# A tuned kernel's stated order of steps is written anew, and the zero products fill TensorE's whole array

## The chip, the core and the metric

The kernel runs on one core of a Trainium2 chip. The core has five engines that run side by side: TensorE (PE, matrix products), VectorE (DVE), ScalarE (ACT), GpSimd (POOL) and SyncE (SP, which here only issues DMAs). Each engine executes its own instructions strictly in the order in which they stand, and an instruction that needs another engine's result waits for it on a semaphore. The metric is the device time of one execution in microseconds (us). Three runs of the kernel before gave 550.38, 552.77 and 553.58 us, so the median is 552.77.

## What is computed

The reference has two stages. The first is a delta rule, for 4 batches and 8 heads, 768 steps and a head width of 48 (`k_n` is the normalised key):

```
y[t]   = q[t] @ state
v_old  = k_n[t] @ state
state += beta[t] * outer(k_n[t], v[t] - v_old)
```

The second takes `x`, which is y with the heads side by side (4 x 768 tokens of 384), and adds a two-layer block to it: `xn = (x - mean)/sqrt(var + 1e-6) * g_ln`, and `out = x + max(xn @ w_ch1, 0) @ w_ch2`, with `w_ch1` of 384 x 1536 and `w_ch2` of 1536 x 384. Everything is float32.

## The kernel before, in words

The 768 steps are cut into 12 chunks of 64 (`C = 64`, `NCH = 12`). A chunk of the delta rule becomes a set of small products of 48 or 64 rows, 32 products to a step, one for each pair of batch and head. They can be told in the profile by their lines:

- L766 (`products`): the chunk's products of keys with keys (`G`) and of queries with keys (`P`);
- L718 and L733 (`first_inverse`, steps `E1` to `E5` and `Z1` to `Z5`): chunk 0's triangular inverse by five rounds of products, each round passing through VectorE (L723 copies under a mask, L683 transposes) and ScalarE (L677 copies);
- L884, L889 (`blocks_join`), L921, L927 (`join`): the inverses of the later chunks, 32 x 32 products that put together what VectorE worked out row by row (`rows_inverse`, L850 and L857);
- L974 (`state` in `recur`: `ks`, `qs`), L993, L998, L1010 and L1029 (`u`), L1046 (`state_up`), L1036 (`out_y`): the recurrence from chunk to chunk. Each chunk reads the state that the chunk before has left.

A layer norm follows (L1080 to L1092) and the chunk's 256 tokens are turned (L1124, or through a DMA). The two-layer block (`mlp`) then runs as large products with 128 rows and 128 columns: L1296 and L1318 for chunk 0 and, in the first layer, chunks 1 and 2; L1229 (`eleven`, the first layer of chunks 3 to 11 with eleven block products instead of twelve) and L1394 (`seven`, the second layer of chunks 1 to 11 with seven for eight). Their sums and differences are done by VectorE (L1251, L1412), GpSimd (L1380, L1419) and ScalarE (L1248).

The order of all this is no scheduler's work at run time. Every step is recorded with `add` in the object `line` (class `Line`): an engine, a function that issues the step's instructions, and what it reads and writes. There are 3154 steps. `Line.emit` then calls them in the order that the string `ORDER` states, number by number, and asserts that no step comes before one that it needs. `a:b` in the string is a range of steps, and `z` is no step but a call of `line.filler`. With `in_this_order` that order becomes the order of each engine's queue, DMAs included.

`line.filler` is the function `zeros` (L1471 to L1473): two products whose result nobody reads, put into columns 384 to 512 of bank `f_[0]`. In the kernel before there are 20 `z`. Their stationary operand is `pmask` (128 rows, 64 columns), so their result covers 64 partitions. The bank `f_[0]` is also one of the banks of `first_inverse`, which uses its columns 0 to 256.

What sets the order around the change is thus the string alone. A product in float32 is issued as two weight loads and two matmuls, a transpose (L576, L1124) as one of each.

Of the kernel before, what the change touches and what calls it, by code (L numbers as in the profile page):

```python
# [16 lines left out]
C = 64  # L17
# [42 lines left out]
8 55 54 47 65 53 59 1 9 10 61 50 52 11 51 2 5 12 32 57 13 74 23 41 29 0 56 66 35 58 37 6 7 48 38 63 75 39 64 42 68 45 76 43 67 91 40 251 92 81 77 80  # L60
93 84 250 36 100 85 33 30 101 102 31 4 34 103 18 78 26 14 17 69 19 15 104 82 105 86 83 87 94 98 27 71 95 28 96 88 99 106 79 97 16 89 107 90 109 24 25
209 113 110 108 111 310 114 112 115 118 204 208 213 119 125 116 72 120 205 z 121 123 122 126 70 128 z 127 117 258 21 124 20 235 22 130 259 129 252 233
256 49 131 46 221 136 255 132 223 44 206 253 142 135 133 137 260 134 138 308 141 222 143 144 139 224 140 238 145 146 632 73 633 148 152 240 234 147
309 236 154 158 149 254 153 151 60 150 257 159 155 160 157 393 156 237 396 161 163 z 219 162 307 3 168 207 169 z 167 210 217 164 392 173 165 211 170
175 166 212 171 261 229 176 178 z 174 172 177 402 244 179 180 321 262 263 186 215 181 320 311 182 242 397 187 192 264 185 265 319 188 184 312 266 183
239 322 189 193 194 190 241 191 401 313 195 196 391 314 246 389 267 200 268 214 315 z z 400 197 243 203 269 218 198 394 270 202 271 201 220 395 272
225 273 274 333 z 248 399 216 275:277 398 278 245 316 334 279 199 280 317 336 281 282 62 331 283 318 338 247 323 357 332 324 z 249 325 341 326 335 z
342 227 284 337 285 327 286 362 287 339 346 355 z z 340 347 328 226 288 343 289 329 348 290 344 356 345 330 291 353 390 367 292 349 293 422 z 294 295
351 352 296 230 350 297 463 231 423 z 354 298 232 425 464 570 358 465 228 462 572 571 365 574 424 363 467 426 469 573 364 360 359 576 366 427 575 466
# [12 lines left out]
690 790 z z 789 691 791 692 792 926 793 564 1187 794 795 1170 890 796 927 891 1188 800 797 902 1183 565 798 1373 801 799 928 693 802 1067 803 807 z z  # L82
z z 694 804 805 1563 930 806 808 1073 810 809 566 695 878 569 892 929 568 1071 567 903 696 1075 697 931 698 1565 699 964 1189 1369 905 700 966 1380
# [123 lines left out]
def kernel(  # L207
# [13 lines left out]
    nc = tc.nc  # L221
# [20 lines left out]
    def sb(name, shape, dt=FP32):  # L242
        return const.tile(shape, dt, name=name)
# [38 lines left out]
    ident = sb("ident", [128, 128])  # L282
    pmask = sb("pmask", [128, C])
# [26 lines left out]
    f_ = [psum.tile([128, 512], FP32, name=f"f{i}") for i in range(4)]  # L310
# [1160 lines left out]
    def zeros():  # L1471
        for _ in range(2):
            nc.tensor.matmul(f_[0][0:C, 384:512], pmask, pmask[:, 0:1].to_broadcast([128, 128]))  # L1473
# [139 lines left out]
```

## Time and profile before

| | before |
|---|---|
| median of three runs | 552.77 us |
| the profiled execution | 553.62 us |
| its span, first to last instruction | 551.9 us |
| mean granted clock of TensorE | 0.974 |
| TensorE matmuls, weight loads | 10088, 10088 |
| busy: TensorE, VectorE, GpSimd, ScalarE | 517.1, 360.4, 254.6, 197.2 us |
| instruction packets for TensorE (queue q8) | 79, 1.29 MB |

The profile is a page and a trace of one execution. Times in it start at the first instruction. Its second part cuts the span into 40 equal slices and gives a digit for each, the busy share in tenths; the row PEclk is the clock that TensorE was granted. A row of waits names the engine and line that waited, what released it, the total, how often and the longest. "issue" as a releaser means that the engine waited for nothing that the profile shows. In rows in order of time the first number is the start, the second the duration of the group; matmuls overlap, so the time that a step takes is read from start to start. "x64" counts matmuls in a trace row.

### The profile page before, as it was taken

To read this page: it belongs to the slowest core of one execution; us is meant where nothing else is said; L and a number is where in the kernel's file an instruction comes from. 1 tells how busy PE (TensorE), PEld (TensorE's weight loads), DVE (VectorE), ACT (ScalarE), POOL (GpSimd) and SP (SyncE) were. 2 spreads that over 40 slices of the span, in tenths; PEclk is the share of its full clock that TensorE was granted. 3 is DMA by queue.
4 is the path that set the end of the run, shared out by engine and by line. 5 is a ranking of instruction groups with operands and counts; after the bars stand their busy time and mean duration, and the time that the engine had idled before them with its cause. 6 is when DMAs were issued, how large, how long until landed. Compare 5 with 4: busy or idle time off the path is not lost.

```text
span 551.9 us, 23155 instructions
## 1 busy us (share of the span) xinstructions
PE 517.1 (94%) x10088; PEld 471.2 (85%) x10088; DVE 360.4 (65%) x884; ACT 197.2 (36%) x496; POOL 254.6 (46%) x399
## 2 busy tenths in 40 slices
PE   7778996999989998998999899999999999999996
PEld 4667884779978897997998899998899998999996
DVE  5668468981789736998758788659858334444331
ACT  5576644341323324223314324223422234132220
POOL 6134184537723697466272444460251551335443
PEclk9687899999999999999999899999999999999999
DMA  9884869178454686452673255761534510303101
GB/s 160 251 182 88 243 146 156 24 172 132 69 71 84 190 135 68 90 102 47 178 107 62 34 107 136 177 90 23 103 60 97 119 19 4 89 1 87 30 1 29
DMA packets 195973, 54.67 MB, mean 99 GB/s; under 512 B 186136, under 2 KB 189344, under 8 KB 195872
## 3 DMA queue, kind: packets, MB, share of 16 engines
q1 hardware_dynamic: 190112, 40.39, 38.4%
q10 hardware_dynamic: 3552, 9.63, 5.6%
q0 software_dynamic: 2208, 3.17, 3.9%
q8 instruction: 79, 1.29, 1.0%
q14 instruction: 22, 0.18, 0.1%
HBM read 36.38 MB, written 16.78 MB: 96 GB/s over the span
## 4 chain that ended last, share of the span: by engine, by line
PE 74%; DVE 10%; issue 5%; DMA 4%; SPq 3%; POOL 1%; ACT 1%; POOLq 0%; ACTq 0%; DVEq 0%
PE f L1229 23%; PE f L1394 22%; PE f L1296 6%; SPq L357 3%; PE two L766 3%; PE f L1318 3%; DVE xb L857 3%; DVE tmp L850 2%; PE by L1036 2%; PE two L1029 2%; PE by L974 2%; PE two L974 2%; PE two L1046 1%; PE f L1473 1%; DMA words<-in_moe_w_ch_dram 1%
## 5 line engine op out<-in xcount | busy, mean ns | idle before, releaser
L1380 POOL TENSOR_TENSOR h_all<-h_all 128x256 f32<-128x256 f32 x99 | 75.7, 770 | 58.0 <-PE f L1394 53.5
L1394 PE MATMUL f<-w_sb,h_all 128*128 128x192 f32 x396 | 95.8, 331 | 1.4 <-issue 1.1
L1229 PE MATMUL f<-xnt,w_sb 128*128 128x128 f32 x648 | 89.8, 280 | 1.3 <-issue 1.0
L1394 PE MATMUL f<-words,h_all 128*128 128x192 f32 x396 | 86.2, 329 | 0.0
L1419 POOL TENSOR_TENSOR words<-h_all 128x128 f32<-128x128 f32 x66 | 30.3, 477 | 120.4 <-ACT h_all L1248 114.6
L1229 PEld LDWEIGHTS f<-xnt,w_sb 128*128 128x128 f32 x648 | 81.6, 194 | 2.9 <-ACT rstd L1086 1.3
L1251 DVE TENSOR_TENSOR h_all<-f,h_all 128x256 f32<-128x256 f32 x135 | 56.1, 419 | 41.1 <-PE f L1229 33.4
L850 DVE TENSOR_TENSOR tmp<-xb,gb 128x60 f32<-128x60 f32 (+19 forms) x170 | 67.4, 396 | 4.5
L1394 PEld LDWEIGHTS f<-w_sb,h_all 128*128 128x128 f32 x396 | 66.4, 190 | 3.3 <-issue 2.0
L857 DVE TENSOR_TENSOR xb<-xb,tmp 128x60 f32<-128x60 f32 (+19 forms) x170 | 65.7, 387 | 3.9
L1394 PEld LDWEIGHTS f<-words,h_all 128*128 128x128 f32 x396 | 67.2, 190 | 0.8 <-POOL h_all L1380 0.2
L357 POOL DMA_DIRECT2D tb<-in_k_dram x64 | 41.9, 658 | 24.2 <-DVE tmp L850 17.0
L1296 PE MATMUL f<-xnt,w_sb 128*128 128x256 f32 x216 | 49.8, 384 | 0.9 <-ACT h_all L1305 0.9
L1296 PEld LDWEIGHTS f<-xnt,w_sb 128*128 128x128 f32 x216 | 40.2, 190 | 7.3 <-ACT h_all L1305 1.3
L1412 DVE TENSOR_TENSOR o<-f,x 128x192 f32<-128x192 f32 x33 | 11.4, 353 | 50.2 <-PE f L1394 40.0
L1248 ACT ACTIVATE h_all<-f 128x256 f32<-128x256 f32 x54 | 20.5, 382 | 65.0 <-PE f L1229 31.7
L1394 PE MATMUL f<-w_sb,words 128*128 128x192 f32 x132 | 32.7, 332 | 1.4 <-DVE o L1412 1.4
L1248 ACT ACTIVATE h_all<-h_all 128x256 f32<-128x256 f32 x54 | 21.4, 412 | 23.0 <-DVE h_all L1251 22.7
L550 POOL TENSOR_TENSOR w_sb<-words 128x768 uint32<-128x768 uint32 (+1 forms) x11 | 15.1, 1374 | 21.1 <-DVE words L537 14.8
L1305 ACT ACTIVATE h_all<-f 128x256 f32<-128x256 f32 x36 | 13.1, 383 | 33.0 <-PE f L1296 33.0
L1394 PEld LDWEIGHTS f<-w_sb,words 128*128 128x128 f32 x132 | 22.8, 190 | 2.0 <-DVE o L1412 1.7
L1074 ACT COPY x<-by 128x384 f32<-128x384 f32 x23 | 10.1, 481 | 30.9 <-PE by L1036 18.1
(235 smaller groups left out, 924.0 us busy)
## 6 DMA issues: line engine op xcount, KB each, us to landing
words<-in_moe_w_ch_dram ACTq DMA_DIRECT2D x10, 768.0 KB, 8.2
gd<-gsb SPq DMA_DIRECT2D x11, 512.0 KB
v<-in_v_dram SPq DMA_DIRECT2D x24, 192.0 KB, 3.7
out_dram<-o SPq DMA_DIRECT2D x48, 96.0 KB, 2.3
kr<-in_k_dram SPq DMA_DIRECT2D x46, 96.0 KB, 3.3
xld<-xlt SPq DMA_DIRECT2D x9, 384.0 KB, 2.5
xnt<-xld SPq DMA_DIRECT2D x36, 96.0 KB, 3.1
gb<-gd SPq DMA_DIRECT2D x40, 64.0 KB, 3.6
```

What stands on the lines that cost most here:

```text
L357: add(eng, cost, lambda: QUEUE[eng].dma_start(out=out_, in_=in_), r, w, bulk=n * ns / 16e3, **kw)
L766: nc.tensor.matmul(pair[hp][half(e ^ (hp & n)), (g * NP + j) * C : (g * NP + j + 1) * C], kt[drows(hp), l], rt[drows(hp), i],)
L850: lambda j=j, n=n, w=w, t=t: nc.vector.tensor_tensor(out=t, in0=xv[:, 0:n, j : j + 1].to_broadcast([128, n, w]), in1=gv[:, j : j + 1, j + ...
L857: "DVE", dve(n * w), lambda t=t, rest=rest: nc.vector.tensor_tensor(out=rest, in0=rest, in1=t, op=ALU.subtract),
L974: nc.tensor.matmul(dst[half(e), hp, j], src[drows(hp), (e if n else key_half(c, hp, e)) * GP + j], s_all[drows(hp), e, j], start=(n == 0 o ...
L1229: nc.tensor.matmul(wide(p[:, 128 * n : 128 * n + 128]), w[:, f : f + 128], r, start=start and n == 0, stop=stop, skip_group_check=True)
L1248: add("ACT", act(256), lambda: nc.scalar.activation(to[0], p, ACTF.Relu), pk, to[1])
L1251: add("DVE", dve(256), lambda: nc.vector.tensor_tensor(out=to[0], in0=ps(p), in1=y[0], op=op), [*pk, *y[1]], to[1])
L1296: nc.tensor.matmul(p[:, 0:TOK], w1_sb[:, t, f * 128 : (f + 1) * 128], xnt[:, t], start=(t == 0), stop=(t == KC - 1))
L1380: add(eng, cost, lambda: e.tensor_tensor(out=out_, in0=x, in1=y, op=op), r, w, port=2 if eng == "Pool" else 1, pr=-2)
L1394: lambda f=f, t=start and f == 0: nc.tensor.matmul(p[:, 0:D2], lhs(f), rhs[:, f], start=t, stop=(f == F2 - 1), skip_group_check=True),
L1419: lambda f=f + i: e.tensor_tensor(out=s3[f], in0=one(0, 0)[0](f), in1=one(1, 0)[0](f), op=ALU.subtract),
```

## The change

Two things change. The whole string `ORDER` is replaced by another permutation of the same 3154 steps, with 21 `z` where there were 20. And `zeros` multiplies other operands: `ident` (128 x 128) is the stationary operand and its first column, repeated 128 times, the moving one, and the result goes to all 128 partitions of the same columns of `f_[0]`.

```
 ORDER = """
-8 55 54 47 65 53 59 1 9 10 61 50 52 11 51 2 5 12 32 57 13 74 23 41 29 0 56 66 35 58 37 6 7 48 38 63 75 39 64 42 68 45 76 43 67 91 40 251 92 81 77 80
...
+8 55 54 47 66 53 59 10 9 6 52 11 7 13 65 57 5 50 61 18 23 51 58 74 0 251 14 1 56 64 27 20 12 24 43 37 75 63 41 38 68 44 67 48 91 49 76 39 92 40 77 93
...
 """

     def zeros():
         for _ in range(2):
-            nc.tensor.matmul(f_[0][0:C, 384:512], pmask, pmask[:, 0:1].to_broadcast([128, 128]))
+            nc.tensor.matmul(f_[0][:, 384:512], ident, ident[:, 0:1].to_broadcast([128, 128]))
```

What the new string does to TensorE's queue is seen when both programs are built and their products listed, line and count. Three places, each before and after:

```
the rounds of first_inverse (E: L718, Z: L733, P: L766, z: a zero pair; 16 products a step)
before  P E1 P z E1 z Z1 Z1 E2 E2 Z2 Z2 E3 E3 Z3 z Z3 z E4 E4 z Z4 Z4
after   P P E1 E1 Z1 z z Z1 E2 E2 Z2 Z2 E3 E3 Z3 z Z3 E4 z E4 Z4 z Z4

chunk 6's recurrence (products)
before  L974:32 L1029:32 L1229:10 L1036:32 L1046:32 L1229:2 L921:32 L1229:10
after   L974:32 L1029:32 L1229:8 L1036:32 L1229:12 L921:32 L1046:32 L1229:4

chunk 8 to chunk 9 (products)
before  L1229:2 L1046:32 L921:32 L1229:26 L766:32 L927:32 L1229:10 L974:64 L1394:2
after   L1229:10 L1046:32 L921:32 L1229:18 L766:32 L1229:10 L974:32 L927:32 L1394:4
```

The other engines' queues hold the same instructions as before, in another order.

More of the change, by code (lines that the diff above doesn't have):

```diff
@@ L59 @@
 ORDER = """
[L60 to L67, printed above, removed]
@@ L68 @@
-342 227 284 337 285 327 286 362 287 339 346 355 z z 340 347 328 226 288 343 289 329 348 290 344 356 345 330 291 353 390 367 292 349 293 422 z 294 295
-351 352 296 230 350 297 463 231 423 z 354 298 232 425 464 570 358 465 228 462 572 571 365 574 424 363 467 426 469 573 364 360 359 576 366 427 575 466
[12 rows of a table removed]
-690 790 z z 789 691 791 692 792 926 793 564 1187 794 795 1170 890 796 927 891 1188 800 797 902 1183 565 798 1373 801 799 928 693 802 1067 803 807 z z
-z z 694 804 805 1563 930 806 808 1073 810 809 566 695 878 569 892 929 568 1071 567 903 696 1075 697 931 698 1565 699 964 1189 1369 905 700 966 1380
[74 rows of a table removed]
+8 55 54 47 66 53 59 10 9 6 52 11 7 13 65 57 5 50 61 18 23 51 58 74 0 251 14 1 56 64 27 20 12 24 43 37 75 63 41 38 68 44 67 48 91 49 76 39 92 40 77 93
@@ new lines @@
+35 78 42 79 100 36 60 101 69 94 81 95 84 96 25 80 26 102 85 103 33 29 32 71 17 19 104 15 86 16 83 87 105 88 82 4 30 31 34 106 21 98 89 90 99 107 113
+109 108 97 110 119 310 111 28 112 114 204 115 116 118 205 120 211 213 72 125 121 123 124 126 128 70 258 127 117 259 122 129 130 z z 223 253 256 132
+214 260 22 136 134 308 133 221 131 140 138 142 135 222 255 137 139 224 210 233 143 144 209 141 45 238 145 146 46 73 632 152 147 208 235 148 633 257
+150 234 149 309 236 151 158 219 154 393 153 250 159 307 160 156 157 212 254 155 161 225 390 163 z 237 162 3 396 252 164 169 165 206 175 166 z 240 171
@@ new lines @@
+170 2 176 167 402 168 177 174 178 207 172 392 173 215 239 320 180 z 179 217 321 261 242 262 322 181 186 263 244 182 389 311 264 265 312 400 267 185
+266 192 184 188 241 394 183 187 189 193 395 194 190 z z 313 391 191 195 246 319 196 268 243 401 314 200 z 269 270 197 245 398 202 201 397 203 315 199
+271 198 272 273 229 274 333 275 316 276 277 317 278 279 230 248 323 318 334 324 227 218 331 280 220 281 326 336 z z 282 332 325 216 283 338 284 357
+285 335 62 286 341 247 327 z z 287 337 288 249 342 362 339 346 328 340 343 289 355 329 290 347 344 345 330 348 226 291 349 292 356 353 z z 293:295 367
@@ L158 @@
+354 296 423 297 351 465 350 422 352 399 570 424 298 231 462 425 572 464 232 363 463 228 466 365 426 z 571 358 427 574 469 573 370 467 359 468 576 364
[11 rows of a table added]
+962 786 675 676 1186 867 677 869 1185 897 678 787 679 1183 886 878 680 898 1076 681 887 682 899 683 888 z 684 685 790 686:688 788 z 792 689 1078 791
+690 1075 795 564 900 562 691 1073 889 796 789 1077 901 800 563 890 1066 902 801 793 891 926 z 794 802 797 561 798 799 927 807 803 565 z z z 810 692
[75 rows of a table added]
 3151:3153
@@ L1472, in zeros @@
         for _ in range(2):
-            nc.tensor.matmul(f_[0][0:C, 384:512], pmask, pmask[:, 0:1].to_broadcast([128, 128]))
+            nc.tensor.matmul(f_[0][:, 384:512], ident, ident[:, 0:1].to_broadcast([128, 128]))
     line.filler = zeros
```

172 rows, old and new, of the table ORDER are left out of this document.

## The prediction

> **What bounds the kernel now.** I read the page first, then TensorE's waits after the opening 60 us, then single places in order of time. From the page:
>
> ```profile
> PE 517.1 (94%) x10088; PEld 471.2 (85%) x10088; DVE 360.4 (65%) x884; ACT 197.2 (36%) x496; POOL 254.6 (46%) x399
> ...
> PEclk9687899999999999999999899999999999999999
> ...
> q8 instruction: 79, 1.29, 1.0%
> ...
> PE 74%; DVE 10%; issue 5%; DMA 4%; SPq 3%; POOL 1%; ACT 1%; POOLq 0%; ACTq 0%; DVEq 0%
> ```
>
> TensorE (PE) is busy for 517.1 of the 551.9 us span; the profiled execution took 553.62 us, 0.85 above the median of the three runs (552.77). So a gain is looked for in the 35 us in which PE is idle and in the slices where its clock is below 9. Queue q8 carries instructions: 1.29 MB in 79 packets, 16.3 KB each, and 10088 matmuls with 10088 weight loads over 79 packets are 255 instructions a packet. I call such a packet a block: 256 instructions, which is 64 of the program's products (each appears as two weight loads and two matmuls; transposes as half of that).
>
> PE's waits from 60 us to the end, by what ended them (total, times, longest):
>
> ```profile
> PE by L889 <- issue: 2.3, 1, 2.3
> PE by L974 <- issue: 2.2, 1, 2.2
> PE two L766 <- issue: 2.1, 2, 1.1
> PE by L921 <- issue: 2.0, 2, 1.4
> PE f L1394 <- DVE o L1412: 1.4, 1, 1.4
> PE f L921 <- issue: 1.2, 1, 1.2
> PE f L1394 <- issue: 1.1, 2, 0.7
> PE f L1229 <- issue: 1.0, 1, 1.0
> PE two L974 <- issue: 1.0, 1, 1.0
> PE f L1296 <- ACT h_all L1305: 0.9, 1, 0.9
> PE f L927 <- issue: 0.9, 1, 0.9
> PE f L1229 <- DVE h_all L1251: 0.7, 2, 0.5
> PE two L1046 <- issue: 0.5, 1, 0.5
> ```
>
> The reader should see that what ends most of these is no engine: "issue" has 14.3 us of them. The one at L1229 (1.0) falls as VectorE ends an L1251, so I leave it out; 13.3 us remain, in 12 places. All but the two longest lie where small products stand close together. One such place, at 309 us, in order of time:
>
> ```profile
> 306.50 1.15 PE L1036 MATMUL by<-u,pt 64*64 64x48 f32 x64
> 307.47 0.90 PE L1046 MATMUL two<-u,kr 64*48 64x48 f32 x64
> 308.30 0.71 PE L1229 MATMUL f<-pt,w_sb 128*128 128x128 f32 x4
> 308.94 0.38 PE L921 MATMUL by<-xnj,gsb 32*32 32x32 f32 x20
> 310.73 0.59 PE L921 MATMUL by<-xnj,gsb 32*32 32x32 f32 x44 [1.41 <-issue]
> ```
>
> PE stops in the middle of a step whose first products had already run, so no operand was missing. From start to start a small step of 32 products (64 matmuls) takes 0.83 to 0.97 us here. Stretches from one such stop to the next, and around two changes of the clock (columns: PE busy and matmuls, weight loads, VectorE, ScalarE, GpSimd, granted clock, DMA share):
>
> ```profile
> 86.93:93.40 6.47, 4.26 (x129) 2.75 (x129) 5.13 (x9) 2.96 (x5) 2.07 (x2) 1.00 0.78 134
> 154.06:158.34 4.28, 3.22 (x128) 2.85 (x128) 3.49 (x9) 1.72 (x5) 0.00 (x0) 1.00 0.78 102
> 244.70:246.76 2.06, 2.06 (x131) 2.01 (x131) 1.92 (x5) 0.14 (x1) 0.97 (x2) 1.00 0.84 113
> 307.82:311.23 3.41, 2.00 (x118) 1.69 (x108) 3.13 (x8) 0.76 (x2) 3.10 (x4) 1.00 0.54 73
> 311.23:314.65 3.42, 3.42 (x25) 3.41 (x17) 1.72 (x4) 0.67 (x2) 0.00 (x0) 0.50 0.12 17
> 17.69:31.34 13.65, 12.50 (x320) 11.00 (x324) 7.41 (x20) 8.90 (x22) 4.93 (x8) 0.50 0.80 224
> ```
>
> From stop to stop PE issues 128 weight loads and 128 matmuls: exactly one block. I read the stop as PE having used up a block before the next has come: that takes 4.3 us at 154 us and 6.5 us at 87 us, where DMA is busier. A block of small steps alone runs in 2 to 3 us. The third row speaks for care: 256 instructions in 2.06 us without a stop, behind a long run of large products, so a fetch also gets a head start.
>
> **The change part by part.** (1) *The order, as to blocks.* Both built programs can be laid out in blocks from their start. Prices: a small step (L766, L974, L1029, L1036) about 1.05 us, L1046 0.83, L921 and L927 0.7 (estimate from 44 matmuls in 0.51 us above), and for the large products:
>
> ```profile
> 492.08 12.55 PE f L1229 x112
> ...
> 506.06 11.38 PE f L1394 x70
> ```
>
> 12.55/112 is 0.112 a matmul, 0.224 a product of L1229 (128 columns); 11.38/70 gives 0.325 a product of L1394. By their columns (256 and 384) a product of L1296 is put at 0.45 and one of L1318 at 0.67, estimates both. Then, for the 12 blocks that end in a stop (block's end; its content in products and its price before; the same place after):
>
> ```
>  us   wait  before                                price  after                                    price
>  84   2.31  884:48 1318:2 1296:3 889:10            3.7   884:50 1296:3 1318:3 889:7               4.3
>  91   2.21  889:54 1318:4 974:5                    3.9   889:57 1318:6                            5.1
> 153   0.53  1029:29 1394:5 1046:30                 3.4   1029:28 1394:6 zero:2 1036:28            4.2
> 157   1.06  1036:32 zero:4 766:26                  2.9   1046:32 zero:2 1394:6 766:20            4.1
> 161   0.96  766:6 1394:3 927:32 974:23             2.6   766:12 zero:8 1124:3 927:32 974:9        3.8
> 207   0.36  974:30 927:32 1394:2                   2.4   927:32 974:30 1394:2                     2.3
> 212   1.21  1394:5 1229:2 1029:32 921:25           3.3   1394:5 1229:4 1029:32 921:21             3.8
> 217   0.85  921:7 1229:8 1036:32 927:17            3.3   921:11 1229:6 1036:32 927:14             2.9
> 309   1.41  1036:20 1046:32 1229:2 921:10          2.2   1036:17 1229:12 921:32 1046:3            4.0
> 383   0.64  1036:22 1229:2 1046:32 921:8           2.2   1036:24 1229:10 1046:30                  3.8
> 399   0.70  974:60 1394:2 1229:2                   3.1   927:31 1394:12 1229:2 974:19             5.6
> 465   1.03  1229:4 927:32 766:28                   2.4   1229:10 927:32 766:22                    3.7
> ```
>
> If the fetch takes as long as before, a stop shrinks by what its block gains in price. Left are 1.7, 1.0, 0.5, 0.7 and 1.3 us at 84, 91, 207, 212 and 217 us, and nothing at the others: 5.2 of 13.3, a gain of 8.1 us. Other blocks of the new order are priced 3.1 us or more, and blocks of 3.1 to 3.7 us passed without a stop before; they stay at nothing. Bounds: 13.3 if all stops go, 0 if something else holds PE in the same places.
>
> [...]
>
> (2) *The clock behind 311 us.* After the window with 1.41 us of waiting the granted clock is 0.50 for 3.42 us, while PE is busy throughout. With the stop gone PE stays busy there and those 25 matmuls take half: 1.7 us gained. Bounds 0 and 1.7.
>
> [...]
>
> (3) *The opening 60 us.*
>
> ```profile
> PE by L733 <- issue: 2.6, 2, 2.0
> PE by L1010 <- issue: 2.0, 1, 2.0
> PE f L718 <- issue: 1.8, 1, 1.8
> PE f L733 <- issue: 0.8, 1, 0.8
> ```
> ```profile
> 20.50 0.78 DVE L723 COPY_PREDICATED gsb<-u,f 128x256 f32<-128x256 int32 x2 [2.94 <-PE f L1473]
> ```
>
> The blocks here are as dense after as before (2.2 to 3.0 us by price), so the 5.2 us of stops at L718 and L733 stay. What changes is the zero products. Before, two stand between the E1 product in bank f0 and VectorE's copy of it, and the copy waited 2.94 us for them, since they write the same bank; after, copies of that product stand ahead of any zero product. That is up to 2.9 us on the chain, but the next Z1 products cross the end of a block, whose stop then ends last. The clock is half in 17.69 to 31.34 us and PE is 12.5 of 13.65 us busy: fully warm it would save at most 6.3 us, but ScalarE (8.90) and VectorE (7.41) alternate with PE in this chain, so little of it comes. The zero products now cover 128 columns of the array for 64; whether that counts for the clock, no row of before shows. None stands between Z1 and Z3 now, so I don't expect the half clock to go. I take a gain of 1 us, between a loss of 3 (a further cold stretch) and a gain of 8.
>
> (4) *The zero products' own price.*
>
> ```profile
> L1473 PE MATMUL f<-pmask 128*64 128x128 f32 x80 | 13.4, 307 | 0.0
> ```
>
> One more pair (21 for 20), four matmuls of 128 columns as an L1229 step has: 0.45 us, where PE waits for others anyway. 0 to 0.45; I take 0.4. That each loads 128 columns of weights costs nothing, as the L1229 steps load as many at their price.
>
> (5) *All else that moves.* GpSimd, VectorE, ScalarE and the DMA queues issue the same instructions in another order. Counted in the two orders, nine steps in ten move on their own queue by at most 4 places on PE, 6 on VectorE, 5 on ScalarE, 8 on GpSimd and 18 among SP's 394 DMAs; the fetches of weights on ScalarE's queue keep their order. A DMA set behind one that still waits for its source is held with it on SP, but no transfer ends one of PE's waits above, so I cost that at nothing. Switches between small and large steps are as many as before (139 for 138 after the opening). A small step often stands later behind five L1229 steps (2.2 us), so consumers get their operands closer: operands that stand under 1.5 us of PE work ahead of their use, their own duration taken off, rise from 410 to 437 of 924. The waits for engines were 1.4, 0.9 and 0.7 in the rows above; I add 1 us, between -2 and +10.
>
> Sum from 553.6: -8.1 -1.7 -1 +0.4 +1 = -9.4, 544.2; on the scale of the median 543.4. I say 544.
>
> **The rivals.** *Waits take the stops' place.* VectorE is 10% of the chain and 5.13 of 6.47 us busy at 87 us. If PE, once it isn't stopped, waits for VectorE instead, only the terms at 309 us and later, where PE bounds plainly, remain: 1.41+0.64+0.70+1.03, 3.8 less the 1.4 of (4) and (5): about 551. For it: VectorE is 3.1 of 3.4 us busy at 308 us. Against it: PE's waits on VectorE are 2.1 us in those 13 rows.
>
> *Fetch isn't the cause*, the stops stay wherever they were: 552, with 1 us either way. Against it stands the count of 256. [...]
>
> *Slower: the recurrence becomes late.* The new order puts five L1229 steps (2.2 us) between state steps (L1029, L1036, L1046) of a chunk, twice a chunk. Each chunk's chain then ends up to 4.5 us later. If in the stage from 150 to 300 us PE has no other work left by then, each chunk costs 4.5 us against a gain of 9.4; it decides from the third chunk on, so three chunks give 553.6 - 9.4 + 13.5 = 557.7. For it: VectorE's share is highest there. Against it: PE's longest wait for an engine was 1.4 us.
>
> *The opening gains too*: 6 us more from warm windows and freed copies, 538.
>
> **Chances.** The forecast (540 to 548) 0.56, opening gains too 0.14, waits take the place 0.12, fetch not the cause 0.05, slower 0.13. This kernel's three runs span 0.6%, so 0.5% is about what tells a change from none: 550.0 to 555.5 is the same. Faster: 0.56+0.14 and a little of the first rival, 0.72; same 0.15; slower 0.13. The range holds 8 in 10 from 536 (most of the opening's 8 us) to 555 (both rivals of no change); the forecast's own is 540 to 548.
>
> **What would show it.** Right: PE's "issue" waits behind 60 us fall from 14.3 to about 6 us, those left lie at L884/L889 and near 207 to 217 us; no half clock near 311 us; PE busy up to 96%. Wrong: issue waits gone but waits for VectorE or ScalarE above 8 us; or issue waits as long as before in other places, which would say that a fetch's length hangs on DMA traffic more than on a block's content; or the opening, up to the first L1296, ending more than 3 us away from where it ended before.

## The result and the profile after

The changed kernel takes 545.96 us (median of four runs, 545.63 to 546.29), the kernel before 552.88 (550.38 to 553.58) beside it: a ratio of 0.988, 95% interval 0.985 to 0.992. In a second session with other runs beside it, it came to 0.991 (0.989 to 0.993). The prediction was 544 us. The profiled execution took 546.29 us, 7.3 less than that of before.

From the page after (busy time of each engine; TensorE's granted clock in 40 slices; the chain that ended last):

```profile
PE 513.4 (94%) x10092; PEld 469.0 (86%) x10092; DVE 369.6 (68%) x884; ACT 197.6 (36%) x496; POOL 253.3 (47%) x399
...
PEclk9888899999999899999999999999999999999999
...
PE 73%; DVE 14%; issue 4%; DMA 3%; ACT 3%; POOL 2%; SPq 0%; ACTq 0%; DVEq 0%; POOLq 0%
```

Of the 7.3 us, 3.7 are PE's busy time (517.1 to 513.4: 27.3 us of the span ran at half clock before, 17.1 after, the stretch in which it ends aside) and 3.6 its idle time. VectorE (DVE) issues the same 884 instructions and is busy 9.2 us longer; its share of the chain rises from 10 to 14%.

PE's waits in the changed kernel from 66 us on (what PE waited for: total, times, longest):

```profile
PE f L1296 <- ACT h_all L1305: 2.5, 1, 2.5
PE two L766 <- DVE s_all L1056: 2.4, 2, 1.8
PE f L1229 <- DVE o L1412: 1.7, 1, 1.7
PE f L921 <- issue: 1.2, 2, 0.9
PE by L889 <- issue: 1.2, 1, 1.2
PE f L1394 <- DVE o L1412: 0.8, 2, 0.6
...
PE f L927 <- issue: 0.4, 1, 0.4
PE f L1229 <- issue: 0.4, 1, 0.4
```

The two sums to take from this list, for this kernel and for before (the same list, over the same stretch): waits ended by "issue" fall from 14.3 to 3.2 us, and waits for other engines rise from 3.3 to 10.7. So 11.1 us were gained and 7.4 of them came back as waits for VectorE, ScalarE and GpSimd. The largest of the new waits, in order of time on three engines:

```profile
177.47 1.16 PE L766 MATMUL two<-kt 48*64 48x64 f32 x64
181.09 5.84 PE L1296 MATMUL f<-xnt,w_sb 128*128 128x256 f32 x18 [2.46 <-ACT h_all L1305]
```
```profile
180.47 0.29 ACT L1086 ACTIVATE rstd<-mv,eps 128x1 f32<-128x1 f32 x1 [3.80 <-DVE mv L1081]
180.67 0.64 ACT L1305 ACTIVATE h_all<-f 128x256 f32<-128x256 f32 x2
```
```profile
172.84 2.50 DVE L857 TENSOR_TENSOR xb<-xb,tmp 128x240 f32<-128x240 f32 x1
```
```profile
173.11 1.01 POOL L1185 TENSOR_TENSOR q_last<-w_sb 128x384 f32<-128x384 f32 x1
174.06 1.00 POOL L1185 TENSOR_TENSOR pt<-w_sb 128x384 f32<-128x384 f32 x1
```

The same L857 in the kernel before:

```profile
174.08 0.41 DVE L857 TENSOR_TENSOR xb<-xb,tmp 128x240 f32<-128x240 f32 x1
```

Read from GpSimd upwards: GpSimd (POOL) runs sums back to back, a VectorE operation beside them takes 2.50 us for its usual 0.41, the statistics L1081 come late, ScalarE waits 3.80 us for them in its square root L1086, and the evictions L1305 queued behind that root hold up PE. The windows around it (PE busy and matmuls, weight loads, VectorE, ScalarE, GpSimd, granted clock, DMA share):

```profile
178.83:182.24 3.41, 1.15 (x5) 1.05 (x6) 3.27 (x10) 1.77 (x5) 1.06 (x2) 1.00 0.02 5
182.24:185.65 3.41, 3.41 (x9) 2.70 (x9) 3.14 (x12) 0.29 (x2) 1.04 (x2) 0.50 0.63 218
```

PE was busy for 1.15 of 3.41 us, and the next 3.41 us ran at half clock. The half clock at 311 us is gone; this one has taken its place.

### The profile page after: what moved, and what is told of

Read it like the earlier page. It is cut to its first block, busy times and chain, and to the rows that moved or that the text cites. A ratio compares the mean times of both kernels' runs of the same rounds, so it can differ in the third digit from the quotient of the medians.

```text
span 544.6 us, 23178 instructions
## 1 busy us (share of the span) xinstructions
PE 513.4 (94%) x10092; PEld 469.0 (86%) x10092; DVE 369.6 (68%) x884; ACT 197.6 (36%) x496; POOL 253.3 (47%) x399
## 3 DMA queue, kind: packets, MB, share of 16 engines
q0 software_dynamic: 2208, 3.17, 3.6%
## 4 chain that ended last, share of the span: by engine, by line
PE 73%; DVE 14%; issue 4%; DMA 3%; ACT 3%; POOL 2%; SPq 0%; ACTq 0%; DVEq 0%; POOLq 0%
PE f L1394 24%; PE f L1229 24%; PE f L1296 6%; DVE xb L857 5%; DVE tmp L850 5%; PE two L766 3%; PE f L1473 2%; PE by L974 2%; DMA words<-in_moe_w_ch_dram 2%; PE two L974 2%; PE by L1036 2%; PE two L1029 1%; PE two L1046 1%; DMA kr<-in_k_dram 1%; PE by L921 1%
## 5 line engine op out<-in xcount | busy, mean ns | idle before, releaser
L1380 POOL TENSOR_TENSOR h_all<-h_all 128x256 f32<-128x256 f32 x99 | 74.9, 760 | 79.6 <-PE f L1394 54.0
L1394 PE MATMUL f<-w_sb,h_all 128*128 128x192 f32 x396 | 96.1, 330 | 0.9 <-DVE h_all L1251 0.4
L1229 PE MATMUL f<-xnt,w_sb 128*128 128x128 f32 x648 | 88.4, 277 | 1.2 <-DVE h_all L1251 0.5
L1394 PE MATMUL f<-words,h_all 128*128 128x192 f32 x396 | 87.3, 329 | 0.0
L1229 PEld LDWEIGHTS f<-xnt,w_sb 128*128 128x128 f32 x648 | 80.5, 192 | 2.7 <-DVE words L1412 0.7
L1251 DVE TENSOR_TENSOR h_all<-f,h_all 128x256 f32<-128x256 f32 x135 | 56.5, 420 | 32.4 <-PE f L1229 25.1
L857 DVE TENSOR_TENSOR xb<-xb,tmp 128x60 f32<-128x60 f32 (+19 forms) x170 | 72.4, 426 | 4.2
L850 DVE TENSOR_TENSOR tmp<-xb,gb 128x60 f32<-128x60 f32 (+19 forms) x170 | 71.5, 421 | 4.1
L1394 PEld LDWEIGHTS f<-w_sb,h_all 128*128 128x128 f32 x396 | 66.8, 190 | 2.6 <-POOL h_all L1380 0.8
L1394 PEld LDWEIGHTS f<-words,h_all 128*128 128x128 f32 x396 | 67.1, 190 | 0.8 <-POOL h_all L1380 0.2
L1412 DVE TENSOR_TENSOR o<-f,x 128x192 f32<-128x192 f32 x33 | 11.6, 354 | 63.0 <-PE f L1394 30.1
L1296 PE MATMUL f<-xnt,w_sb 128*128 128x256 f32 x216 | 51.0, 392 | 2.5 <-ACT h_all L1305 2.5
L1296 PEld LDWEIGHTS f<-xnt,w_sb 128*128 128x128 f32 x216 | 41.5, 195 | 9.3 <-ACT h_all L1305 2.6
L1248 ACT ACTIVATE h_all<-f 128x256 f32<-128x256 f32 x54 | 20.4, 381 | 65.2 <-PE f L1229 38.2
L1394 PE MATMUL f<-w_sb,words 128*128 128x192 f32 x132 | 33.0, 332 | 0.6 <-DVE o L1412 0.6
L550 POOL TENSOR_TENSOR w_sb<-words 128x768 uint32<-128x768 uint32 (+1 forms) x11 | 15.0, 1360 | 36.2 <-DVE words L537 23.2
L1305 ACT ACTIVATE h_all<-f 128x256 f32<-128x256 f32 x36 | 13.2, 382 | 33.2 <-PE f L1296 32.8
L1394 PEld LDWEIGHTS f<-w_sb,words 128*128 128x128 f32 x132 | 22.9, 190 | 1.0 <-DVE o L1412 0.7
```

The lines of the kernel that those rows point to most:

```text
L850: lambda j=j, n=n, w=w, t=t: nc.vector.tensor_tensor(out=t, in0=xv[:, 0:n, j : j + 1].to_broadcast([128, n, w]), in1=gv[:, j : j + 1, j + ...
L857: "DVE", dve(n * w), lambda t=t, rest=rest: nc.vector.tensor_tensor(out=rest, in0=rest, in1=t, op=ALU.subtract),
L1229: nc.tensor.matmul(wide(p[:, 128 * n : 128 * n + 128]), w[:, f : f + 128], r, start=start and n == 0, stop=stop, skip_group_check=True)
L1248: add("ACT", act(256), lambda: nc.scalar.activation(to[0], p, ACTF.Relu), pk, to[1])
L1251: add("DVE", dve(256), lambda: nc.vector.tensor_tensor(out=to[0], in0=ps(p), in1=y[0], op=op), [*pk, *y[1]], to[1])
L1296: nc.tensor.matmul(p[:, 0:TOK], w1_sb[:, t, f * 128 : (f + 1) * 128], xnt[:, t], start=(t == 0), stop=(t == KC - 1))
```

## The experiments

All times are ratios to the kernel before, measured beside it. The waits are PE's from 66 us on in the profiled execution, summed from its list of waits as above; "first L1296" is the start of the first L1296 product, the end of the opening.

```
kernel                               ratio (95%)             issue  engines  first L1296
before                               1                       14.3    3.3     65.2
changed                              0.988 (0.985 to 0.992)   3.2   10.7     63.0
changed, second session              0.991 (0.989 to 0.993)   3.5    9.9     61.0
old order, new zeros                 1.004 (1.000 to 1.007)  11.1    3.0     67.2
new order, old zeros                 0.992 (0.989 to 0.995)   3.7    8.5     61.5
old order, half a block on           0.994 (0.991 to 0.998)   7.3    5.8     63.5
new order, half a block on           1.003 (0.999 to 1.006)   8.9    7.5     65.3
old order, a whole block on          1.011 (1.007 to 1.014)   9.4    3.8     67.8
root behind evictions                0.992 (0.989 to 0.995)   0.9   15.6     60.8
sums later                           0.990 (0.987 to 0.993)   2.1   10.6     61.1
32 by 32 zeros                       0.991 (0.987 to 0.994)   2.0   15.9     62.0
four waits moved                     0.999 (0.996 to 1.002)   0.8   15.2     59.8
wait filled with zeros               0.988 (0.984 to 0.992)   2.1    7.7     61.0
sums and reads moved                 0.992 (0.989 to 0.995)   0.8   14.8     59.7
```

**Which part carries it: order or zero products.** The old order with the new zero products:

```diff
-            nc.tensor.matmul(f_[0][0:C, 384:512], pmask, pmask[:, 0:1].to_broadcast([128, 128]))
+            nc.tensor.matmul(f_[0][:, 384:512], ident, ident[:, 0:1].to_broadcast([128, 128]))
```

> The old order with the new zero products (128 weight rows by 128 columns in place of 128 by 64), nothing else. Theory (the order carries the gain, through the instruction blocks): the stops ended by issue after 60 us stay at 14.3 us within 1, and the time stays within 1.5 us of before. Rival (the zero products carry it, through the clock of the opening 60 us): the half-clock stretches of the opening become shorter, the first product of L1296 comes 2 to 4 us sooner than at 65.2 us, and the time falls by 2 to 4 us.

The new order with the old ones (the same diff the other way round):

> The new order with the old zero products. Theory (order): as the changed kernel, stops ended by issue after 60 us at 3.2 us within 1, time within 1.5 us of 546. Rival (zero products): the opening is 2 to 4 us longer than in the changed kernel, the time 548 to 550; the stops after 60 us stay at 3.2 all the same.

The first came out at 1.004, the second at 0.992, as fast as the changed kernel within the intervals. So the order carries the gain. The first kernel's waits ended by issue were 11.1 us instead of 14.3 within 1; they still stand at blocks that had them before. Its first L1296 came 2 us later, not sooner, so the rival's condition did not come either.

**The blocks: shift without moving a step.** One pair of zero products ahead of the first L1296 becomes 34 tiny products, 128 instructions more, half a block. The tokens of the order stay, but for that one:

```diff
-... 230 350 297 463 231 423 z 354 298 232 ...
+... 230 350 297 463 231 423 y 354 298 232 ...
+    def tiny():          # token y
+        for _ in range(34):
+            nc.tensor.matmul(f_[0][0:32, 384:416], pmask[0:32, 0:32], pmask[0:32, 0:1].to_broadcast([32, 32]))
```

> The old order; the last pair of zero products ahead of the first L1296 (at 64.6 us) is replaced by 34 products of 32 by 32, so that everything behind it stands 128 instructions, half a block, later in the blocks; no step is moved. Theory (PE runs out of a block of 256 instructions): by the same prices as in the prediction the sum of what blocks fall short of 3.5 us goes from 11.6 to 2.4 us, so most of the 13.3 us of stops ended by issue goes, to 3 to 6 us, and the time falls by 6 to 8 us (the small products themselves cost 0.2 more than the pair they replace). Rival 1 (the stops belong to the steps where they stand: their operands, banks or semaphores): stops at the same steps, time within 1 us of before. Rival 2 (waits for engines take the stops' place): issue falls as in the theory, waits for VectorE and ScalarE rise by as much, time within 2 us of before.

The same at 62 us of the new order (with ident for pmask):

> The new order with the same shift by half a block at its 62 us. Theory (blocks): the sum by prices rises from 2.2 to 11.1 us; stops ended by issue after 66 us rise from about 3 to 9 to 14 us, at places that had none, and the time rises by 5 to 8 us to 551 to 554: the order's gain is lost without a step being moved. Rival 1 (steps): nothing changes, within 1 us of 546. Rival 2 (waits for engines take turns with stops): issue rises but waits for engines fall by about half of it, time up by 2 to 4 us.

And the control, 66 tiny products in the old order, which shift by a whole block:

> The control for the shift by half a block: the old order, the same pair of zero products replaced by 66 products of 32 by 32 in place of 34, so that everything behind stands 256 instructions, one whole block, later and every block has the content that it had. Theory (content of the blocks): stops ended by issue after 66 us at 13 to 14.5 us again, in the places of before, and the time 1 to 2 us above before (the 66 products cost about 1.7 us where the pair cost 0.55). Rival (the half-block kernel was faster for another reason, such as the small products themselves or a later start): stops at 7 us as there and time 2 to 4 us below before.

The half block takes the old order from 1 to 0.994, and the new order from 0.988 or 0.991 back to 1.003. PE's waits for issue in these two kernels (old order, half a block on; then new order, half a block on):

```profile
PE by L889 <- issue: 3.1, 1, 3.1
...
PE by L1036 <- issue: 2.1, 2, 2.0
```
```profile
PE f L884 <- issue: 3.9, 1, 3.9
PE by L1036 <- issue: 1.8, 2, 1.3
...
PE f L1229 <- issue: 1.6, 2, 0.9
PE two L1046 <- issue: 1.1, 1, 1.1
```

In the old order every stop behind 160 us is under 0.5 us, but for the L1229 that the prediction left out (at 255.85 us, 1.04); in the new order there are stops at 160, 317 and 341 us (1.07, 0.74 and 0.34), places that had none. The control, in order of time:

```profile
159.59 0.45 PE L766 MATMUL two<-qt,kt 48*64 48x64 f32 x12 [1.33 <-issue]
...
216.10 0.32 PE L921 MATMUL f<-xnj,gsb 32*32 32x32 f32 x13 [1.48 <-issue]
...
313.83 0.59 PE L921 MATMUL by<-xnj,gsb 32*32 32x32 f32 x44 [0.86 <-issue]
400.55 0.59 PE L1394 MATMUL f<-w_sb,h_all 128*128 128x192 f32 x2 [0.72 <-issue]
467.79 0.49 PE L766 MATMUL two<-qt,kt 48*64 48x64 f32 x7 [1.30 <-issue]
```

Before had stops at L766 (158.34 us, 1.06), L921 (213.00, 1.21), L921 (310.73, 1.41), L1394 (399.59, 0.70) and L766 (466.42, 1.03): the same steps, the middle of the steps included (the L921 at 311 us again goes on with 44 matmuls). Shifted by a whole block, ten of the twelve stops come back (those at 162 and 384 us, 0.96 and 0.64, do not); shifted by half, nearly all go. That rules out the steps' own operands, banks and semaphores, and the tiny products themselves. The control's total is 9.4 and not 13 to 14.5: a stop's length varies from one execution to the next where its place does not. The one at L889 took 2.3 us in before, 1.7 in the old order with new zeros and 0.7 in the control; in the two profiles of the changed kernel the one at L927 took 0.4 us in the first and none was left in the second.

Two further signs stand in the traces. Take all of TensorE's recorded instructions from the program's start (matmuls, weight loads and its semaphore instructions) and number them. In the 14 profiles PE has 149 waits ended by issue from 10 us on, and at 133 of them the number leaves the same remainder when it is divided by 256, in both orders and whatever the shift. Of the other 16, 14 are the wait at L1229 that the prediction left out, once in each profile. The second sign is queue q8: ahead of each of the 64 stops of these kernels behind 66 us, an instruction packet of 16 KB ends, as a rule 1.1 to 1.8 us before PE goes on (once 2.2). In before, such a packet runs from 308.33 to 309.20 us, and PE goes on at 310.73. The packets themselves take 0.9 to 1.9 us. What sets the time at which one is asked for is not shown.

Three things in these runs are not as the theory had them. The old order kept 7.3 us of issue waits instead of 3 to 6 (3.1 of it at L889 at 87 us, where the prices gave none), and only about half of the 7.0 us saved was seen in the time: waits for engines rose from 3.3 to 5.8, with a new one of 2.65 us at L1296 for L1305, at the place where the changed kernel has one too. PE's products ahead of it start 3.2 us sooner than in before, VectorE's L1081 that the wait hangs on only 1.4 us sooner. The expectation's second rival holds for that part. The tiny products also took 2.3 us where the pair took 0.6. In the new order the time rose by more than its waits for issue less the waits for engines (5.7 less 3.2): its PE was busy 518.4 us instead of 513.4, for the tiny products (2.3 us) and for matmuls at half clock (from 82.5 to 89.4 us, around the stop of 3.9). And the control is slower than before by more than was expected, 1.011: its 66 tiny products ran for 4.3 us where 1.7 were put, and behind 66 us it had 13.7 us at half clock where before had 3.4.

**The zero products' size.** As many instructions, next to no array use:

```diff
-            nc.tensor.matmul(f_[0][:, 384:512], ident, ident[:, 0:1].to_broadcast([128, 128]))
+            nc.tensor.matmul(f_[0][0:32, 384:416], ident[0:32, 0:32], ident[0:32, 0:1].to_broadcast([32, 32]))
```

> The changed kernel with its zero products cut from 128 by 128 to 32 by 32: as many instructions, so that every block keeps its content, but next to no use of the array. Theory (zero products matter little, as before's sort against the new sort did): time within 1.5 us of the changed kernel, stops ended by issue after 60 us at 3.2 us within 1. Rival (they keep the clock up): the mean granted clock falls below 0.975, half-clock stretches are added in the opening and at 160 us, and the time rises by 2 to 5 us.

The mean granted clock did fall, to 0.964 to 0.981 in six executions, where the unaltered kernel beside it had 0.980 to 0.984:

> The changed kernel unaltered, so that the other kernels of this study have it beside them on one chip with as many runs. Every theory: 0.988 of before, within its interval (0.985 to 0.992), 543 to 549 us.

But the time stayed: 0.991 for 0.991. In this profile 17.1 us of the opening ran at half clock, 6.8 in the unaltered kernel's beside it and 13.7 in that kernel's first profile. So the mean clock was lower with the tiny zero products, and the time did not show it.

**The wait at 178 us, attacked three ways.** First the queue place: the root goes behind the two evictions.

```diff
-... 991 942 719 977 1579 1383 981 720 ...
+... 991 719 977 1579 1383 981 942 720 ...
```

> The changed kernel with one step of ScalarE moved: the square root L1086 (step 942), which waited 3.8 us for VectorE's L1081 with two evictions L1305 (steps 977, 981) queued behind it, goes behind both. No other engine's order changes. Theory (PE's longest wait, 2.46 us at 178.6 us, comes from this one queue place): the wait goes to under 0.5 us, the half-clock stretch at 182.2 us goes with it, and the time falls by 2.5 + 1.7 = 4.2 us at most, 2 to 4 by the median. Rival (VectorE's chain sets the pace there): PE waits as long a few steps later, at L1124 or L766, for VectorE, and the time stays within 1 us of the changed kernel.

Then its source: the three sums of GpSimd go behind step 986.

```diff
-... 1568 715 963 716 ... 937 961 936 ... 979 958 938 ... 945 986 1070 ...
+... 1568 715 716 ... 937 936 ... 979 938 ... 945 986 963 961 958 1070 ...
```

> The changed kernel with three steps of GpSimd moved: the sums L1185 (steps 963, 961, 958), which ran back to back at 173.1 to 176.2 us, go behind step 986, to about 183 us where GpSimd idled 4.8 us. ScalarE's order stays. Theory (GpSimd's operations hold up VectorE's beside them): VectorE's L857 of 128 by 240, 2.50 us there against 0.41 before, takes under 0.8 us; L1081 ends 1.5 to 2.5 us sooner, PE's wait of 2.46 us shrinks to under 1 us, the half clock at 182.2 us goes, and the time falls by 2 to 4 us; VectorE's operations at 183 to 186 us become longer instead. Rival (the 2.5 us has another cause, such as the DMA transfers then): L857 stays at about 2.5 us and the time within 1 us.

Both took the wait at 178 us away (the first left 1.05 us at an L1394; in the second L857 of 128 by 240 is back to 0.55 us), and neither moved the median from the changed kernel's: 0.992 and 0.990. In both, a wait of 1.9 to 2.0 us that had been 0.3 stood some 25 us later, and the half clock with it (209.6 to 219.8 us in the first, 203.6 to 207.0 in the second). From the second's waits, then its VectorE and GpSimd in order of time:

```profile
PE f L1229 <- POOL qt L1210: 2.0, 1, 2.0
```
```profile
177.70 3.48 DVE L857 TENSOR_TENSOR xb<-xb,tmp 128x156 f32<-128x156 f32 x1
```
```profile
178.09 1.01 POOL L1185 TENSOR_TENSOR q_last<-w_sb 128x384 f32<-128x384 f32 x1
179.05 1.00 POOL L1185 TENSOR_TENSOR pt<-w_sb 128x384 f32<-128x384 f32 x1
180.01 0.99 POOL L1185 TENSOR_TENSOR qt<-w_sb 128x384 f32<-128x384 f32 x1
```

The moved sums now hold up another L857, for 3.48 us, until the last sum ends: GpSimd's operation is what stretches VectorE's, in both places. The first kernel's 15.6 us of waits for engines hold another one besides. At 78 us PE waits 3.4 us at L884 for a transpose of VectorE, which itself waits for a DMA:

```profile
77.91 0.71 DVE L878 STREAM_TRANSPOSE xnj<-xt 128x512 f32<-128x512 f32 x1 [3.71 <-DMA tb<-in_q_dram]
```

This wait, 2.5 to 3.4 us, stands in four of the 14 profiles (those with 14.8 to 15.9 in the column "engines") and not in the other ten, among them both of the changed kernel, from which three of the four differ only behind this place. A sum of waits from one profile carries such draws; the medians decide.

I then took the wait at 203 us away too, by putting SP's reads xnt (952 to 954) ahead of four reads gb:

> The changed kernel with the three sums of GpSimd moved, as in the kernel that had only that, and the three reads xnt ahead of the four reads gb on SP's queue; VectorE's and ScalarE's order untouched. Theory (queue places): no wait of over 1 us at 178 and 203 us, the half clock at 203.6 us goes, time 541 to 544 us, 0.982 to 0.986 of before. Rival (the next hand-over is late by as much): a wait of 1 to 2 us within 10 us behind 203 us, time within 1.5 us of the changed kernel's 0.991.

0.992 again, and the next hand-over was late (PE 2.70 us for VectorE's L1412 at 209.6 us). With two more VectorE edits, an update L1056 and two evictions L1412 ahead of row operations of the inverse:

```diff
-... 524 525 ... 652 ... 435 ...
+... 434 435 ... 524 525 ... 652 ...
-... 1136 1332 1137 ... 1139 ... 1140 ... 1329 ... 1141 1398 1353 ... 1354 ...
+... 1136 1329 1332 1137 ... 1398 1353 1354 1139 1140 1141 ...
```

> The changed kernel with four waits for engines attacked, TensorE's and ScalarE's order untouched. The three sums of GpSimd go behind step 986 as in the kernel before this one; on SP's queue the three reads xnt (steps 952 to 954) go ahead of four reads gb (GpSimd's L1210 waited for them, PE 2.0 us at 203.5 us, as soon as the wait at 178 us was gone); on VectorE the update L1056 (step 435) goes ahead of a transpose and three row operations (PE waited 1.79 at 110 us), and two evictions L1412 (steps 1329, 1354) ahead of the row operations at 250 us (1.73 + 0.35). Theory (these waits are queue places, and PE is the bound behind them): waits for engines after 66 us fall from 10 to under 5 us, half-clock stretches after 66 us to one or none, and the time to 538 to 542 us, 0.974 to 0.982 of before. Rival (the chain through VectorE and DRAM sets the pace there, and a wait taken away comes back at the next hand-over): new waits of 2 to 4 us in all, time 544 to 547, within 2 us of the changed kernel.

This one lost nearly all of the gain, 0.999. Two of its waits:

```profile
113.55 1.02 PE L1124 MATMUL by<-ident,xln 128*128 128x128 f32 x6 [2.42 <-DVE xln L1092]
...
260.18 1.22 PE L1229 MATMUL f<-xnt,w_sb 128*128 128x128 f32 x4 [3.17 <-DVE h_all L1251]
```

In the changed kernel PE waited 1.79 us at 110 us (L766, for the update L1056) and 0.58 at 113 us (L1124), 2.37 in all; with the update put forward the first wait is gone and the second is 2.42. The wait was moved, not removed: VectorE's work up to that point was the same, and it has next to no idle time there (busy 13.05 of the 13.50 us up to 113.5). At 250 us the evictions put ahead delayed row operations and an L1251, and 1.73 became 3.17. So the theory of queue places falls; the rival, a chain through VectorE, holds in these stretches. A third wait, 3.44 us at L884 at 78 us, is the draw told above. Behind both of the waits shown the clock is half (115.4 to 118.8 and 258.8 to 265.6 us), and over twelve executions the mean clock was 0.965 to 0.981, where the unaltered kernel had 0.980 to 0.984. How much of the lost gain is the clock's was not isolated.

Last, the clock by itself: two zero products of 128 by 512 inside the wait at 178 us, no step moved.

```diff
-... 720 721 1381 982 994 ...
+... 720 721 1381 y 982 994 ...
+            nc.tensor.matmul(f_[1], ident, ident[:, 0:1].to_broadcast([128, 512]))   # token y, twice
```

> The changed kernel with two more zero products, of 128 by 512, ahead of the L1296 that waits 2.46 us for ScalarE at 178.6 us (step 982); they write a bank that is free and whose old content is no longer read. They add eight instructions. Theory (a clock period at half speed follows a window of 3.41 us in which the array was used little, and costs 1.7 us): the half-clock stretch at 182.2 us goes, the wait itself shrinks to 0.5 to 0.9 because the zeros stand in it, and the time falls by 1 to 2 us against the changed kernel. Rival (behind that wait the chain through VectorE sets the pace, so that a faster PE only waits later): the half clock goes and the time stays within 0.5 us.

```profile
177.09 1.99 PE L1477 MATMUL f<-ident 128*128 128x512 f32 x4
179.62 4.15 PE L1296 MATMUL f<-xnt,w_sb 128*128 128x256 f32 x18 [0.54 <-ACT h_all L1305]
```
```profile
177.20:180.61 3.41, 2.87 (x9) 1.46 (x10) 3.27 (x10) 1.61 (x4) 0.90 (x2) 1.00 0.00 0
180.61:184.02 3.41, 3.41 (x18) 3.05 (x17) 3.17 (x12) 1.20 (x5) 1.20 (x2) 1.00 0.60 206
```

The 18 matmuls of L1296 take 4.15 us where they took 5.84, 1.7 less, and the granted clock stays at 1.00. The time was 543.54 us, 0.988 (0.984 to 0.992): the lowest median of all the kernels run and faster than before, though its interval overlaps both of the changed kernel's, so that a gain over that one is not shown.

## Why the prediction came out right, and where it did not

The forecast of 544 was 2 us from the median of 546. Its mechanism, the blocks of instructions, was right; the sizes of (1), (2), (3) and (5) were off, and they partly cancelled, so that the number came this close is in part luck.

(1) *The order, as to blocks*: 5.2 us of stops were to be left; 3.2 are, the 0.4 at L1229 included, so the gain was some 10 us for 8.1. They lie where they were put, at L889 (84 us) and L921/L927 (211 and 215 us), except the one of 207 us. This step is shown, by the shift of half a block in both orders, by the control, and by the common remainder and the instruction packets. The prices give the sum roughly (11.1 by prices, 8.9 measured in the shifted new order) but not each place: two of its blocks, priced 2.0 and 2.2, end at 389 and 399 us without a stop, and the one at L884 stopped for 3.9 us where its price of 1.5 gives 2.0. The rival that fetch isn't the cause is ruled out. That DMA traffic makes the longer stops is not shown: in the two rows that the prediction compared, the DMA share is 0.78 in both, and only the rate differs (134 and 102 GB/s). Most blocks end without a stop: behind 66 us, 12 of before's 70 instruction packets are followed by one; those 12 cost 13.3 us of 552.

(2) *The clock behind 311 us*: that stretch is gone, but 182 us has a new one of the same length and price. The filled wait shows the price (1.7 us). What was wrong is to book it as a gain of one place: the second session's profile of the same kernel had half-clock stretches at 179, 210 and 254 us, so their number behind 60 us is a draw from each execution. In the changed kernel PE was busy for 1.15 to 2.04 of the 3.41 us ahead of each of its half-clock stretches, the one in which the span ends aside; in the filled wait it was busy for 2.87 of 3.41 us, and the full clock followed.

(3) *The opening*: put at a gain of 1; mis-sized. The first L1296 began at 65.2, 67.2, 63.5 and 67.8 us in the four profiles of the old order, mean 65.9; in the ten of the new order at 59.7 to 65.3, mean 61.5. Three of these profiles have tiny products just ahead of it (1.7 us more than the pair in the half-block kernels, 3.7 in the control); less these the means are 64.6 and 61.3, a gain of 3.2 (2.2 in the two profiles compared first; my sign for being wrong was more than 3). It doesn't come where the prediction looked for it. The copy that waited 2.94 us for the zero products in its bank did get sooner:

```profile
18.46 0.77 DVE L723 COPY_PREDICATED gsb<-u,f 128x256 f32<-128x256 int32 x2 [1.15 <-PE f L718]
```

The first L733 product starts at 22.2 to 24.6 us in the old order and at 19.1 to 20.5 in the new. But behind the stop of the block that follows, nothing is left of this lead: the step Z3 starts at 32.0 us in the mean of either order. So the discount on this copy, with the block's stop ending last, was right. What the prediction gave no term is the second row of its own list, the 2.0 us at L1010, and behind it stands the mechanism that it had priced, at another copy. Before, PE and then ScalarE:

```profile
46.28 1.11 PE L766 MATMUL f<-kt 48*64 48x64 f32 x64
47.33 1.10 PE L1473 MATMUL f<-pmask 128*64 128x128 f32 x8
50.41 0.87 PE L1010 MATMUL by<-v,xt 64*64 64x48 f32 x32 [1.98 <-issue]
```
```profile
48.52 0.37 ACT L677 COPY xt<-f 128x256 f32<-128x256 f32 x1 [2.81 <-PE f L1473]
```

After, the same:

```profile
43.97 0.71 PE L1473 MATMUL f<-ident 128*128 128x128 f32 x4
44.61 1.16 PE L766 MATMUL f<-kt 48*64 48x64 f32 x64
46.05 0.62 PE L1010 MATMUL by<-v,xt 64*64 64x48 f32 x6 [0.28 <-ACT xt L677]
```
```profile
44.77 0.37 ACT L677 COPY xt<-f 128x256 f32<-128x256 f32 x1 [0.69 <-PE f L1473]
```

L1010 reads `xt`, which ScalarE copies from the last products of the inverse, the first of these copies out of bank `f_[0]`, into which the zero products write. In the old order two pairs of zero products stand behind L766, and the copy waits for them; the copies end at 50.30 us, and L1010 starts at 50.41. In the new order one pair stands ahead of L766, and the copy runs beside L766. From the first product of L766 to this copy the four old profiles take 2.2 to 2.4 us and the ten new ones 0.2; the wait at L1010 is 1.98 us in all four and 0.28 in all ten. (That the list of before puts it to "issue" is an inference of the profile; three of the old profiles put it to GpSimd's L550.) In the mean the new order is 0.3 us ahead at L766 and 3.0 at L1010. A block's stop of up to 1.7 us inside that L1010, in nine of the ten, takes part of it back for a while. No run moved these zero products alone.

(4) *The zero products' price*: 0.4 or nothing; no run can tell them apart. New for old zeros made no gain in either order (1.004 in the old), nor did tiny ones.

(5) *All else that moves*: +1 within -2 to +10; it was +7.4, the largest miss. I had counted leads of operands, which hardly changed, and not what PE does when it is no longer stopped: it runs into VectorE. The old order shifted by half a block shows this without any step moved (3.3 to 5.8). The new order adds GpSimd's sums beside VectorE's row operations. My sign for being wrong, waits for VectorE and ScalarE above 8 us, did come (9.7); my sign for being right, PE busy up to 96%, did not (94%, as before). So the rival "waits take the stops' place" held for two thirds of the gain; that it didn't end at 551 is due to stops that went beyond my count and to the opening.

The measured sum: -11.1 (issue) +7.4 (engines) -2.2 (opening) is -5.9 of the -7.3 between the two profiled executions. Of the other 1.4, 1.1 is PE's busy time behind the first L1296 (464.3 to 463.2 us). The slower rival, a late recurrence, would show at L766's waits for the state's update L1056: 2.4 us in two places, none in before. That is far from 4.5 us a chunk.

## What to carry to other kernels

Count TensorE's instructions from the program's start, semaphore instructions included, and price each block of 256: where a block holds only small products, PE can stop at its end for issue (up to 3.9 us here), and a step moved or 128 instructions added far ahead shifts such stops through the whole program (14.3 to 7.3 us in the old order, 3.2 to 8.9 in the new). Where filler products write a bank that a copy has still to read, the copy waits for them too (2.81 us at the L677 ahead of L1010). Before booking a removed stop as gain, ask which engine is nearly full in that stretch; here waits for other engines, VectorE above all, took back two thirds, and moving single waits on queues moved them on. Where such a wait can't be removed, products of zeros in it can save the half clock behind it (here 1.7 us of PE's time; a gain in the whole time was not shown).

## What the runs showed of the hardware

- VectorE's L857 took longer while GpSimd's tensor operations ran beside it: L857 of 128 by 240 took 2.50 us beside back-to-back sums and 0.41 without, L857 of 128 by 156 took 3.48 beside them and 0.32 in the changed kernel. Both the inputs of L857 are in SBUF. L1056, one of whose inputs is in PSUM, took 0.92 to 0.96 us each time in the profiles of before and of the changed kernel, also at 246.50 us in the latter, where GpSimd's L1380 ran beside it throughout. Whether the place of the input makes this difference was not tested. Both of the long L857 have a recorded start ahead of the first sum's (172.84 and 173.11 us; 177.70 and 178.09).
- In the profiles of before and of the changed kernel the half clock came in stretches of 3.41, 6.83 and 13.65 us (one, two and four times 3.41), the stretch in which the span ends aside. It came at other places in other executions of one kernel: behind 66 us at 182 us in the changed kernel's first profile, at 179, 210 and 254 in its second. Executions of the kernel with the later sums lay between 543.1 us (mean clock 0.991) and 548.3 (0.977).
- With the same order of steps the opening took between 59.7 and 63.0 us in the nine profiles without tiny products (65.3 in the one with them). A comparison of two profiles alone can't tell 2 us there.
